# Clustered attention and a two-layer channel mix: the order of all steps written out as one list, on one core

## The chip, the cores and the metric

The kernel runs on one core of one Trainium2 chip. The metric is device time in microseconds (us) of one execution. The kernel before was timed three times. One more execution was recorded by the hardware profiler; every row of the profile below is of that execution. The engines are TensorE (PE, with its weight loads PEld), VectorE (DVE), ScalarE (ACT), GpSimd (POOL) and SyncE (SP), which here only issues DMAs.

## What is computed

Four batches, eight heads, 768 positions, head width 64, 16 centroids per head; then a mix over positions of rank 32 and a channel mix 512 to 2048 to 512. Cut to what matters:

```python
q_assign = argmax(normed(q) @ normed(centroids).T)       # 16 clusters, k the same
mask     = q_assign[..., :, None] == k_assign[..., None, :]
attn     = softmax(where(mask, 0.125 * q @ k.T, -1e9))
x        = (attn @ v), heads side by side                 # (4, 768, 512)
u        = x + (x.T @ U @ V).T
out      = u + relu(u @ w_ch1) @ w_ch2
```

U, V and the two weight matrices arrive as float64 bits and are joined into float32 on the chip.

## The kernel before

**Attention.** Sixteen steps i, one for each batch and pair of heads (four to a batch). For each: `load` brings q and k (tile R), `split_hi` (ACT) and `split_lo` (POOL or DVE) cut them into a high and a low half, `sims`, `largest` and `clusters` find each position's cluster, `clusters_T` (ACT, tile ohT) turns that into one-hot rows, and `place_clusters` writes these by eight DMAs from SP into the large tile `arena`, where they stand beside q and k as further rows of one matrix product. `rowmax` (L570 PE, L572 DVE) is a first pass over the scores for the row maxima, `rowmax_place` (ACT) puts these into `arena` by a DMA of its own queue (tile mT). Then come `scores` (L594 and L596 on PE, the exponential L599 on ACT), `weights` (L609, sums on POOL and DVE), `values` (L617, the weights times v, matmuls of the form 128*64), and `sums`, `sums_T`, `normalise`. After each fourth step come `mix_u`, `mix_sum`, `mix_v`.

**Channel mix.** `fetch_blocks` (L787) reads u back in blocks, `turn_blocks` (L793) transposes on DVE, `add_u` and `split_u` (L805) make operands; `convert` and `merge` (L219, L220, L222: three DVE instructions for each half tile, called "a conversion" below) join the weights' bits, `split_w` (L828) and `split_w2` (L837) cut them into halves, `stage_w` and `load_w2` bring stored ones back from DRAM. The first product is done with seven products instead of eight for each 2 by 2 block: `product(g, p)`, p = 0 to 6, six matmuls each (L854 to L856, tile ps_h), whose result DVE adds up (L862) or ACT copies (L866). `relu` (L892 DVE, L894 ACT) gives hh and hl, and `gemm2` (L1048 to L1050, tile y) multiplies by the second matrix, with `finish` after it. From group 16 on (the "phase") the second product is done with seven products too: `relu_home`, `add_h`, `split_h` (L922 DVE, L924 ACT), `product2` (L997 to L999, tile z), `combine2` (L1007), `output` (L1030, L1033 and a DMA).

**Order.** Tables of numbers (`times`, `mixes`, `stages`, `joins`, `mlp`, `phase`, `order0`, `paces`, `spots`) give every step a time in units of its own. `at` puts (time, step) into `plan`, the plan is sorted, and each step, when called, emits all its instructions, on all the engines that it uses, at this one place. `keep_order` then pins the order of emission on each engine. So each engine works through its instructions strictly in that order, and one that waits holds everything behind it on that engine.

**Buffers.** A rotating tile is taken from a pool with `bufs=2` or more; which buffer it is follows from the order of the calls.

**Semaphores of the DMAs.** The DMAs of SP and ACT draw from one set of eight completion semaphores in turn. They appear in the lists below as DMAHW0 to DMAHW7. A DMA whose semaphore is still held by an earlier DMA waits for that one to complete.

The places that the change and the prediction touch: `plan`, `at` and the last four lines of `clustered_attention_moe`; `merge`, `convert`; `product`; `place_clusters`, `rowmax_place`; `values`; `split_h`, `output`; `turn_blocks`, `fetch_blocks`; every `tile(...)` of a rotating pool.

## Time and profile before

| what | value |
|---|---|
| three timed runs, median (lowest to highest) | 1012.67 us (1010.91 to 1015.03) |
| the profiled execution, its own time | 1011.91 us |
| its span in the trace | 1009.5 us |
| its mean granted TensorE clock | 0.98 |
| busy: PE, PEld, DVE | 943.9 us (93%), 757.4 us (75%), 781.2 us (77%) |
| busy: ACT, POOL | 463.8 us (46%), 656.8 us (65%) |
| chain that ended last, by engine | PE 64%, DVE 13%, POOL 7%, DMA 6%, issue 4%, ACT 3% |

PE is busy for all but 65.6 us of the span. Matmuls are pipelined, so a busy PE is not a PE at its peak. The clock column gives the share of full speed that was granted; 0.50 is 1.2 GHz and 1.00 is 2.4 GHz. The list of waits says which engine stood still for whom, and the timeline of one engine shows in which order its instructions ran and what stood ahead of the one that was late.

### The profile page before, as it was taken

What the parts mean: (1) busy time and instruction counts of PE and PEld (TensorE: products, weight loads), DVE (VectorE), ACT (ScalarE), POOL (GpSimd) and SP (SyncE); (2) the same over time, 40 slices, a digit from 0 to 9 for tenths busy, and PEclk for the clock granted to TensorE, in tenths of its full rate; (3) what the DMA queues carried; (4) which work ended last, traced back from release to release, by engine and by line L of the source; (5) the groups of instructions that cost most, each with busy time, mean ns of one, the idle gap of its engine ahead of it and who ended that gap; (6) DMA issues with size and microseconds to landing.
All of it is one profiled execution on the core that took longest, in us unless ns stands there. A gap on an engine that the chain in (4) does not pass through costs nothing.

```text
span 1009.5 us, 14837 instructions
## 1 busy us (share of the span) xinstructions
PE 943.9 (93%) x5098; PEld 757.4 (75%) x5098; DVE 781.2 (77%) x1251; ACT 463.8 (46%) x680; POOL 656.8 (65%) x433
## 2 busy tenths in 40 slices
PE   7799999999999999999999899998798997999997
PEld 5566666666667666658888778887698887999996
DVE  5798888778887877567886767665777998588974
ACT  7355555565556545553433334432334453345530
POOL 6467776788678879975688887964723673035620
PEclk9899999999999999999999899999989999999999
DMA  7656656575656665037377765689476966777785
GB/s 199 149 134 173 167 145 189 154 195 148 191 145 178 167 158 126 1 65 205 128 254 256 250 211 196 243 272 257 165 215 152 214 196 185 229 157 164 236 252 136
DMA packets 169645, 183.13 MB, mean 181 GB/s; under 512 B 110426, under 2 KB 119252, under 8 KB 168548
## 3 DMA queue, kind: packets, MB, share of 16 engines
q1 hardware_dynamic: 136672, 156.21, 56.4%
q10 hardware_dynamic: 32900, 25.99, 8.1%
q8 instruction: 40, 0.66, 0.3%
q14 instruction: 33, 0.27, 0.1%
HBM read 112.72 MB, written 41.42 MB: 153 GB/s over the span
## 4 chain that ended last, share of the span: by engine, by line
PE 64%; DVE 13%; POOL 7%; DMA 6%; issue 4%; ACT 3%; SPq 2%; ACTq 1%; POOLq 0%; DVEq 0%
PE o_ps L617 12%; PE ps_max L570 7%; PE st L594 6%; PE st L596 6%; PE ps_h L854 4%; PE ps_h L856 4%; PE ps_h L855 4%; PE z L998 3%; PE z L999 3%; PE z L997 3%; PE y L1050 2%; PE y L1049 2%; PE y L1048 2%; POOL sums_w L820 2%; DVE m L572 2%
## 5 line engine op out<-in xcount | busy, mean ns | idle before, releaser
L609 POOL TENSOR_TENSOR T<-T,pr 128x768 f32<-128x768 f32 x120 | 222.7, 1856 | 52.4 <-DVE T L609 30.7
L572 DVE TENSOR_REDUCE m<-ps_max 128x1 f32<-128x384 f32 x372 | 186.5, 545 | 44.8 <-PE ps_max L570 43.2
L599 ACT ACTIVATE pr<-st 128x768 f32<-128x768 f32 x186 | 148.9, 812 | 74.9 <-PE st L596 63.1
L854 PE MATMUL ps_h<-arena,combos 128*128 128x384 f32 x352 | 122.3, 348 | 14.1 <-DVE rw_g L862 8.4
L617 PE MATMUL o_ps<-pr,vt 128*64 128x384 f32 x768 | 131.1, 490 | 0.7 <-DMA vt<-in_v 0.3
L856 PE MATMUL ps_h<-arena,combos 128*128 128x384 f32 x352 | 120.9, 344 | 5.3 <-POOL combos L944 4.0
L570 PE MATMUL ps_max<-arena 128*128 128x384 f32 x372 | 114.8, 374 | 7.4 <-DMA arena<-ohT 5.5
L855 PE MATMUL ps_h<-arena,combos 128*128 128x384 f32 x352 | 120.6, 343 | 0.5 <-DVE arena L805 0.5
L617 PEld LDWEIGHTS o_ps<-pr,vt 128*64 128x64 f32 x768 | 52.5, 137 | 66.2 <-issue 58.9
L594 PE MATMUL st<-arena 128*128 128x384 f32 x372 | 100.2, 350 | 1.3 <-ACT pr L599 1.3
L570 PEld LDWEIGHTS ps_max<-arena 128*128 128x128 f32 x372 | 67.9, 191 | 41.5 <-issue 14.4
L596 PE MATMUL st<-arena 97*128 97x384 f32 x372 | 95.9, 339 | 0.0
L609 POOL TENSOR_TENSOR T<-pr 128x768 f32<-128x768 f32 x30 | 56.5, 1885 | 46.5 <-ACT pr L599 46.5
L854 PEld LDWEIGHTS ps_h<-arena,combos 128*128 128x128 f32 x352 | 67.9, 193 | 23.5 <-DVE rw_g L862 9.2
L944 POOL TENSOR_TENSOR combos<-rw,combos 128x1024 fp32r<-128x1024 f32 x10 | 24.9, 2490 | 92.7 <-ACT combos L946 92.7
L1050 PE MATMUL y<-w,hl 128*128 128x512 f32 x192 | 78.0, 406 | 3.7 <-DVE hl L892 3.6
L1049 PE MATMUL y<-w,hh 128*128 128x512 f32 x192 | 77.4, 403 | 2.4 <-POOL w L837 2.4
L594 PEld LDWEIGHTS st<-arena 128*128 128x128 f32 x372 | 65.1, 189 | 16.4 <-issue 7.3
L1048 PE MATMUL y<-w,hh 128*128 128x512 f32 x192 | 76.1, 396 | 0.0
L894 ACT ACTIVATE hh<-c 128x768 fp32r<-128x768 f32 x32 | 27.1, 846 | 102.1 <-DVE c L862 100.9
L856 PEld LDWEIGHTS ps_h<-arena,combos 128*128 128x128 f32 x352 | 67.8, 192 | 7.6 <-POOL combos L944 5.7
L855 PEld LDWEIGHTS ps_h<-arena,combos 128*128 128x128 f32 x352 | 68.1, 193 | 4.6 <-DVE arena L805 1.0
(213 smaller groups left out, 2153.3 us busy)
## 6 DMA issues: line engine op xcount, KB each, us to landing
combos<-w_scr SPq DMA_DIRECT2D x112, 256.0 KB
R<-in_qk SPq DMA_DIRECT2D x32, 384.0 KB
arena<-arena SPq DMA_DIRECT2D x64, 192.0 KB
arena<-arena SPq DMA_DIRECT2D x31, 384.0 KB
late_rw<-in_w SPq DMA_DIRECT2D x20, 512.0 KB
u<-u_scr SPq DMA_DIRECT2D x96, 96.0 KB
rw<-w_scr SPq DMA_DIRECT2D x15, 512.0 KB
vt<-in_v SPq DMA_DIRECT2D x16, 384.0 KB
```

The lines of the kernel that those rows point to most:

```text
L570: nc.tensor.matmul(ps[:, 0:HS], x1[:, 0, g // 2, g % 2, t * P:(t + 1) * P], x1[:, 1, h, g % 2, :], start=True, stop=True)
L572: nc.vector.reduce_max(live["m2", i][:, h, u:u + 1], ps[:, 0:HS], axis=AX.X)
L594: nc.tensor.matmul(st[:, j, 0:HS], x1[:, 1, hk, j, ks], x1[:, 0, h, j, :], start=True, stop=False)
L596: nc.tensor.matmul(st[:, j, 0:HS], x2[0:97, 1, hk, j, ks], x2[0:97, 0, h, j, :], start=False, stop=True)
L599: nc.scalar.activation(pr, st[:, :, 0:HS], AF.Exp, scale=SCALE)
L609: eng.tensor_add(T, live["p", i, h, 0] if c == 1 else T, live["p", i, h, c])
L617: nc.tensor.matmul(o_ps[64 * j:64 * j + 64, 0:HS], vv[:, c, j, :], pr[:, j, :], start=(c == 0), stop=(c == NT - 1))
L854: nc.tensor.matmul(ps, ah[:, d], oh[:, d], start=(d == 0), stop=False)
L855: nc.tensor.matmul(ps, ah[:, d], ol[:, d], start=False, stop=False)
L856: nc.tensor.matmul(ps, al[:, d], oh[:, d], start=False, stop=(d == 1))
L1049: nc.tensor.matmul(y, hh[:, f, ts], w2[:, 1, f, :], start=False, stop=False)
L1050: nc.tensor.matmul(y, hl[:, f, ts], w2[:, 0, f, :], start=False, stop=(g in lasts and f == 1))
```

## The change

The time tables go. In their place stand `sequence`, a list of 4,334 step numbers, and `kept`, which holds for each rotating tile a string of buffer numbers. Steps that used more than one engine are written as generators that stop between engines (`@pieces(n)`, `yield`), and `list_work` writes all steps down in a plain order. The list then calls them, a piece at a time, in its own order. The operations and their counts are the same on every engine (4,552 matmuls on PE in both).

```diff
-times = {
-    "load0":           (-38.729, -44.925, -46.182,   None,   None, -82.544),
...
+kept = {
+    "R":
+        "0101010101010101010110101110100110",
...
+def pieces(n):
+
+    def mark(fn):
+        fn.pieces = n
+        return fn
+    return mark
...
+    def place(home, key, shape, dtype, name):
+
+        return home.tile(shape, dtype, name=name, tag=f"{key}{next(turns[key])}", bufs=1)
...
     def merge(rw, g, b, t):
 
         nc.vector.tensor_scalar(b, g, 3, None, op0=ALU.logical_shift_left)
+        yield
         nc.vector.scalar_tensor_tensor(out=b, in0=g, scalar=-0x80000000, in1=b,
                                        op0=ALU.bitwise_and, op1=ALU.bitwise_or)
+        yield
...
+    @pieces(3)
     def product(g, p):
...
-        ps = (work("ps_h") if g <= NG else pool["y"].tile([P, 512], F32, name="ps_h", tag="y"))[:, 0:HS]
+        ps = (work("ps_h") if g <= NG else place(pool["y"], "y", [P, 512], F32, "ps_h"))[:, 0:HS]
...
+        yield
+
         def combine(out, i0, i1, op=ALU.add):
...
+    def put(fn, *args):
+
+        count = getattr(fn, "pieces", 1)
+        plan.extend([fn(*args) if count > 1 else iter(lambda: fn(*args), 0)] * count)
...
-    plan.sort(key=lambda event: event[:2])
-    for _, _, fn, args in plan:
-        fn(*args)
+    list_work()
+    for k in sequence:
+        next(plan[k], None)
     keep_order(tc)
```

What the list does is seen in the engines' own orders. Three places follow. Line numbers differ between the two files: L862 is L1078 after, L922 is L1140, L219, L220 and L222 are L382, L384 and L387, L262 is L429.

**SP in the opening, around `place_clusters` of step 1** (ohT to `arena`); the second list begins at the same `load` of step 2, and R is q and k. Before:

```order
L380 DMA R_487<-in_qk 128x768 [waits DMAHW7_49,PE_49]
L262 DMA arena_124<-arena_124 32x1536 [waits DMAHW1_49,DMAHW0_49]
L262 DMA arena_124<-arena_124 32x1536 [waits DMAHW4_49]
L262 DMA arena_124<-ohT_502 16x384 [waits DMAHW2_49,Activation_49]
L262 DMA arena_124<-ohT_502 16x384 [waits DMAHW3_49]
L262 DMA arena_124<-ohT_502 16x384
L262 DMA arena_124<-ohT_502 16x384 [waits DMAHW5_49]
L262 DMA arena_124<-ohT_502 16x384 [waits DMAHW6_49]
L262 DMA arena_124<-ohT_502 16x384 [waits DMAHW7_49]
L262 DMA arena_124<-ohT_502 16x384 [waits DMAHW0_49]
L262 DMA arena_124<-ohT_502 16x384 [waits DMAHW1_49]
L380 DMA R_487<-in_qk 128x768 [waits DMAHW2_49]
```

After:

```order
L555 DMA R_468<-in_qk 128x768 [waits DMAHW4_49,PE_49]
L555 DMA R_468<-in_qk 128x768 [waits DMAHW5_49]
L429 DMA arena_124<-ohT_472 16x384 [waits DMAHW7_49,DMAHW6_49,Activation_49]
L429 DMA arena_124<-ohT_472 16x384
L429 DMA arena_124<-ohT_472 16x384 [waits DMAHW0_49]
L429 DMA arena_124<-ohT_472 16x384 [waits DMAHW1_49]
L429 DMA arena_124<-arena_124 32x1536 [waits DMAHW2_49]
L429 DMA arena_124<-arena_124 32x1536 [waits DMAHW4_49]
L429 DMA arena_124<-ohT_472 16x384 [waits DMAHW5_49]
L429 DMA arena_124<-ohT_472 16x384 [waits DMAHW6_49]
L429 DMA arena_124<-ohT_472 16x384 [waits DMAHW7_49]
L429 DMA arena_124<-ohT_472 16x384 [waits DMAHW0_49]
```

The first four writes of ohT, for the first half of step 1, now stand ahead of the two row copies of `place_queries`, which are between them and the second four. All eight together stand ahead of the next loads.

**DVE in the channel mix, around the conversion numbered 20** (L219, L220, L222 before; L382, L384, L387 after), which in the kernel before stands between the sums of `product(6, 2)` (tile rw_g) and `product(6, 3)` (tile rw_t); hl is the low half of `relu`. Before:

```order
L862 TENSOR_TENSOR c0_5034<-ps_h_5937,rw_g_5926 128x384
L862 TENSOR_TENSOR rw_g_5965<-ps_h_5958,rw_g_5926 128x384
L219 TENSOR_SCALAR joined_5197<-late_g_5196 128x512
L220 SCALAR_TENSOR_TENSOR joined_5197<-late_g_5196,joined_5197 128x512
L222 SCALAR_TENSOR_TENSOR joined_5197<-late_rw_5195,joined_5197 128x512
L862 TENSOR_TENSOR rw_t_5987<-ps_h_5980,rw_g_5965 128x384
L862 TENSOR_TENSOR c0_5034<-rw_t_5987,ps_h_6002 128x384
L892 SCALAR_TENSOR_TENSOR hl_6019<-c0_5034,hh_6018 128x768
L862 TENSOR_TENSOR rw_t_6029<-ps_h_6022,rw_g_5965 128x384
L862 TENSOR_TENSOR c1_5035<-ps_h_6022,rw_t_5987 128x384
```

After, from the same sum of `product(6, 2)` on:

```order
L1078 TENSOR_TENSOR rw_g_6005<-ps_h_5963,rw_g_5960 128x384
L1078 TENSOR_TENSOR rw_t_6035<-ps_h_6018,rw_g_6005 128x384
L1078 TENSOR_TENSOR c0_5066<-rw_t_6035,ps_h_6027 128x384
L1110 SCALAR_TENSOR_TENSOR hl_6059<-c0_5066,hh_6047 128x768
L1078 TENSOR_TENSOR rw_t_6068<-ps_h_6038,rw_g_6005 128x384
L1078 TENSOR_TENSOR c1_5067<-ps_h_6038,rw_t_6035 128x384
L382 TENSOR_SCALAR joined_5214<-late_g_5213 128x512
L1078 TENSOR_TENSOR c1_5067<-ps_h_6049,rw_t_6068 128x384
L384 SCALAR_TENSOR_TENSOR joined_5214<-late_g_5213,joined_5214 128x512
L387 SCALAR_TENSOR_TENSOR joined_5214<-late_rw_5212,joined_5214 128x512
```

The three instructions of the conversion moved behind four sums of group 6 and its first `relu`, and a sum of `product(6, 6)` stands between the first of the three and the second.

**DVE in the phase, around `split_h` of the operand t3** (tile h_t3, which the first `product2` of that operand needs); the transposes of c1 and the sums into u are `output`. Before:

```order
L1007 TENSOR_TENSOR c0_5034<-z_8089,z0_7418 128x384
L1007 TENSOR_TENSOR c0_5034<-z_8093,z0_7418 128x384
L922 TENSOR_TENSOR combos1_5033<-h_left_7417,combos1_5033 128x768
L1030 STREAM_TRANSPOSE c1_5035<-c0_5034 128x384
L805 TENSOR_TENSOR arena_124<-turned_127,arena_124 128x768
L1033 TENSOR_TENSOR u_7756<-c1_5035,u_7756 128x384
L1030 STREAM_TRANSPOSE c1_5035<-c0_5034 128x384
L1033 TENSOR_TENSOR u_7756<-c1_5035,u_7756 128x384
L922 TENSOR_TENSOR arena_124<-h_t3_7421,arena_124 128x768 x3
```

After:

```order
L1226 TENSOR_TENSOR c0_5066<-z_8065,z0_7406 128x384
L1140 TENSOR_TENSOR arena_124<-h_left_7405,arena_124 128x768
L1140 TENSOR_TENSOR arena_124<-h_t3_7409,arena_124 128x768
L1018 TENSOR_TENSOR arena_124<-turned_127,arena_124 128x768
L1140 TENSOR_TENSOR combos1_5065<-h_left_7405,combos1_5065 128x768
L1140 TENSOR_TENSOR arena_124<-h_t3_7409,arena_124 128x768 x2
L1251 STREAM_TRANSPOSE c1_5067<-c0_5066 128x384
L1018 TENSOR_TENSOR arena_124<-turned_127,arena_124 128x768
L1140 TENSOR_TENSOR arena_124<-h_left_7405,arena_124 128x768
```

The first of the three splits of h_t3 moved ahead of a split of u (L805 before, L1018 after), of the last split of h_left, and of all four instructions of `output`. 

The other moves of a size, in words. On DVE, `turn_blocks(2, 0, 2)` and `turn_blocks(2, 0, 3)` stood ahead of the sum of `product(14, 2)` and now stand behind `relu` of group 14's first half. The split of t1 (L805) and one `split_w` (L828) stood ahead of the sum of `product(15, 4)` and now stand behind it. The `fetch_blocks`, `turn_blocks` and `split_u` of batch 1 moved forward, from the beginning of the channel mix into the last attention steps. On PE, the runs of consecutive `values` matmuls are 59 instead of 33, the runs of `product` 69 instead of 98, and those of `gemm2` 62 instead of 92. On SP, nine of the loads of R and v stand nearer to the step that reads them: between the load of R for step 9's second half, for one, and its `sims` the order of emission has 113 matmuls before and 27 after. For the nine these numbers are 45 to 132 before and 20 to 49 after.

## Rows read from the trace of the kernel before

**Rows 1.** Windows of the span: us, busy us (instructions) by engine, clock, DMA share, GB/s.

```profile
0.00:50.00 50.00, 38.31 (x204) 25.44 (x205) 31.99 (x71) 27.36 (x58) 26.39 (x65) 0.93 0.70 174
50.00:425.00 375.00, 370.88 (x2164) 251.12 (x2164) 307.08 (x611) 207.12 (x310) 293.98 (x162) 1.00 0.58 153
425.00:475.00 50.00, 46.66 (x240) 32.34 (x239) 32.62 (x44) 23.63 (x34) 35.85 (x24) 0.97 0.48 111
475.00:760.00 285.00, 261.75 (x1245) 229.62 (x1244) 210.19 (x266) 106.90 (x139) 200.82 (x135) 0.96 0.69 223
760.00:1010.00 250.00, 226.26 (x1252) 218.87 (x1250) 199.37 (x263) 98.79 (x141) 99.74 (x48) 0.98 0.73 192
```

**Rows 2.** Waits of PE, 475 to 760: tile, line, releaser, us in total, times, longest.

```profile
PE ps_h L854 <- DVE rw_g L862: 8.4, 4, 4.0
PE ps_h L854 <- DVE c L862: 4.6, 2, 4.1
PE ps_h L854 <- DVE rw_t L862: 4.1, 1, 4.1
PE y L1050 <- DVE hl L892: 3.6, 4, 1.7
PE y L1049 <- POOL w L837: 2.4, 1, 2.4
```

**Rows 3.** Waits of PE, 760 to 1010: the first two and the last of seven.

```profile
PE z L998 <- DVE arena L922: 8.1, 4, 4.2
PE ps_h L856 <- POOL combos L944: 4.0, 4, 1.8
...
PE z L997 <- DMA combos<-w_scr: 0.5, 2, 0.3
```

**Rows 4.** Waits of PE, 0 to 50: the first.

```profile
PE ps_max L570 <- DMA arena<-ohT: 5.5, 1, 5.5
```

**Rows 5.** Waits of PE, 425 to 475: the first of seven.

```profile
PE ps_rep L670 <- ACT xu L666: 0.7, 1, 0.7
```

**Rows 6.** Waits of PE, 50 to 425: the first of six.

```profile
PE st L594 <- ACT pr L599: 1.3, 3, 0.7
```

**Rows 7.** Windows of the eight half-clock stretches: two of them, and their sum.

```profile
37.90:44.70 6.80, 5.07 (x13) 3.78 (x13) 4.39 (x9) 0.38 (x1) 0.00 (x0) 0.50 0.66 186
...
563.60:570.40 6.80, 5.56 (x16) 5.29 (x17) 5.72 (x9) 1.41 (x2) 6.41 (x8) 0.50 0.55 210
...
sum 37.50, PE 33.17 PEld 30.30 DVE 25.01 ACT 6.73 POOL 14.91; mean PE 4.15 PEld 3.79 DVE 3.13 ACT 0.84 POOL 1.86
```

**Rows 8.** Timeline of DVE, 553 to 568: start us, us, line, operation, [idle before].

```profile
557.13 1.64 DVE L219 TENSOR_SCALAR joined<-late_g 128x512 int32<-128x512 int32 x1 [2.04 <-ACT late_g L716]
...
564.24 0.55 DVE L862 TENSOR_TENSOR rw_t<-ps_h,rw_g 128x384 f32<-128x384 f32 x1
```

**Rows 9.** Line L222, the last third of a conversion: ns, shortest/median/longest.

```profile
L222 DVE SCALAR_TENSOR_TENSOR joined<-late_rw,joined x8: 692/1114/2758, 514.1 to 593.4; 128x512 int32<-128x512 int32 x8
```

**Rows 10.** Timeline of DVE, 694 to 705.

```profile
701.79 0.58 DVE L793 STREAM_TRANSPOSE turned<-u 128x384 f32<-128x384 f32 x1 [5.61 <-DMA u<-u_scr]
```

**Rows 11.** Waits of SP's DMA queue, 683 to 703.

```profile
SPq L787 <- DMA w_scr<-late_rw: 6.0, 1, 6.0
```

**Rows 12.** Timeline of SP, 27 to 42: eight issues, merged.

```profile
29.73 9.73 SPq L262 DMA_DIRECT2D arena<-ohT  x8
```

**Rows 13.** Waits of SP's DMA queue, 27 to 40.

```profile
SPq L262 <- DMA arena<-mT: 4.9, 1, 4.9
```

**Rows 14.** Timeline of PE, 201.5 to 204.

```profile
202.17 0.52 PE L570 MATMUL ps_max<-arena 128*128 128x384 f32 x2
202.62 1.83 PE L617 MATMUL o_ps<-pr,vt 128*64 128x384 f32 x10
```

**Rows 15.** Timeline of SP, 4.5 to 12.

```profile
4.74 0.58 SPq L380 DMA_DIRECT2D R<-in_qk  x1
```

**Rows 16.** Timeline of ACT, 10.5 to 13.

```profile
11.09 0.83 ACT L461 CAST arena<-R 128x768 fp32r<-128x768 f32 x1 [0.78 <-DMA R<-in_qk]
```

697 lines of the change are left out of this document (335 added, 362 removed), and 207 rows, old and new, of the table sequence.

## The prediction, as it was made before the run

> **What bounds the kernel now.** I read the windows of the span first [rows 1]. The reader is to see that PE is busy nearly throughout: 370.88 of 375 us in attention from 50 on, 261.75 of 285 in the channel mix, 226.26 of 250 in the phase. DVE, the next, has 307.08, 210.19 and 199.37 us there. So PE sets the time, and a reordering that adds and removes no operation can gain only where PE stands still, or where it runs at the lower clock. Second, the list of PE's waits, stage by stage, shows who ends them. In the channel mix five groups make 23.1 us, of which 17.1 are `product` waiting for DVE's sums [rows 2]. In the phase seven make 16.8, led by `product2` waiting for DVE's `split_h` with 8.1 and `product` waiting for POOL's combos with 4.0 [rows 3]. In the opening one wait of 5.5 stands out, for the one-hot rows' DMA [rows 4]. From 425 to 475 seven groups make 3.2 us [rows 5], and in the 375 us of attention six make no more than that, the first with 1.3 [rows 6]: there PE is simply full. Third, the granted clock. It is 0.50 (1.2 GHz, the lower of the two levels) in eight stretches of 37.5 us in all, each right behind a stall of PE; PE is busy for 33.17 us of them [rows 7]. Matmuls that took 33.17 us at half clock would take about half at full, so the low clock itself costs up to 16.6 us. A stall of 4 us therefore costs more than 4.
>
> **The change part by part.** The operations are the same, so no term is for work added or removed. The sum is made against the profiled execution's 1011.91 us, which lies 0.76 below the median of the three runs and 2.4 above its span; I let those 2.4 stand.
>
> *Channel mix, 475 to 760.* The pattern is one engine's queue: DVE works strictly in order, and a conversion of three instructions stands ahead of the sum that frees `product`'s buffer. From 557.13 to 564.24 the conversion holds DVE for 7.1 us [rows 8], and PE stands still for 4.1 of them, up to that sum [rows 2]. So PE could swallow 3.0 us of delay there and not 7.1. In the new order the three instructions come later and, at this one, with a sum between the first and the second. The longest instruction of that kind took 2.758 us [rows 9]: one alone lies within the 3.0. Two together, as the second and third here, can still cost up to 2.5 (twice 2.758 less 3.0), but at the shortest 0.692 nothing. At 701.79 DVE had waited 5.61 us for the DMA of u before `turn_blocks` [rows 10], and `product(14, 2)` was behind it; it now stands ahead. That DMA itself stays late, since SP's issue waited 6.0 for an earlier DMA's completion semaphore [rows 11]; what is late next is then the `split_u` behind the transpose, whose readers come later. The split of t1 and the `split_w` that stood ahead of `product(15, 4)` moved behind it too. Price of all that: 23.1 us of waits, and the low clock. Four of the eight stretches lie here, two of 6.8 and two of 3.4 us; in the first PE is busy for 5.56 of 6.80 [rows 7], at which share the four hold 16.7 busy us and cost half of that, 8.3. Together 31.4. What moved away is nearly everything that I traced a stall to, but each moved piece stands ahead of something else, and DVE is still busy for 74% of the stage. I take 22, about two thirds. Bounds: 31 (the whole), and 8 (only the two clean cases, 4.1 and 4.0, with no clock).
>
> One row speaks against taking all. The same instruction of a conversion took 0.692 us at the shortest and 2.758 at the longest [rows 9], and in the stretch where it was longest POOL was busy for 6.41 of 6.80 us [rows 7]. The Trainium skill, "SBUF — State Buffer", section "Who interferes with whom", says that a DVE instruction with two SBUF inputs contends with a GpSimd instruction that reads SBUF, and that the second to start blocks until the first is done. The trace agrees in its 0.692 against 2.758. By that rule moving the instruction does not make it short, and where the new place has POOL at work it may only move the stall. By the row of the 3.0 us that PE can swallow this term is 22, by the rule at its worst the lower bound, 8: that is the first rival below.
>
> *Phase, 760 to 1010.* Waits of 16.8 us [rows 3], and two half-clock stretches of 3.4 and 3.5 us, worth 2.8 at the same share: 19.6. The longest wait, 4.2 [rows 3], ends with the first `split_h` of t3, which had `output` and two splits ahead of it; it now goes ahead of them. What is late next is `output`, which nothing on PE reads. The POOL waits come from stored weights brought late; two of those loads now go ahead of block loads on SP. But DVE is busy for 80% of this stage [rows 1], so what is put back comes due soon. I take 12, or 60%. Bounds: 19 (nearly the whole) and 4 (the longest wait alone).
>
> *Opening, to 50.* SP's eight writes of one-hot rows take from 29.73 on 9.73 us to issue [rows 12], because one waits 4.9 us for the semaphore of a DMA of ACT's queue [rows 13], and PE loses 5.5 [rows 4]. In the new order the first half stands earlier and no DMA of ACT stands between. To this belongs a half-clock stretch of 6.8 us with 5.07 busy [rows 7], worth 2.5. Together 8.0; ACT's reordered copies may give 1 more or less. I take 6.5; bounds 10 (with 2 from the earlier ACT work) and 2 (the next load holds it).
>
> *425 to 475.* The chain from `sums` to `mix_v` keeps its order. Of 3.2 us of waits [rows 5] and a half-clock stretch of 3.4 us, worth 1.4, I take 1; bounds 5 and 0.
>
> *Attention.* A run of `values` matmuls has another tile form. Entering one, two `rowmax` matmuls take 0.45 us from start to start of the next (202.17 to 202.62) [rows 14] where 2164 matmuls in 375 us make 0.17 each [rows 1], or 0.35 for two: 0.1 more, and about as much at the exit. 26 more runs by 0.2 are 5 us lost, and nothing hides it, since PE is full there. At most 1 us of the waits [rows 6] is won back: +4; bounds 0 and 9 (twice the price, less 1).
>
> The rest (batch 1's blocks fetched in attention, where DMA and DVE have room; buffers named by hand) costs nothing as long as they land in time; DVE's 82% of the stage [rows 1] is the cover, and without it the third rival comes in.
>
> Sum: 1011.91 − 22 − 12 − 6.5 − 1 + 4 = 974.4; with the 0.76 to the median, 975.
>
> **The rivals.** *Gains given back*, about 1000. DVE's pieces remain long beside POOL, and each stall reappears at a neighbour. For it: 0.692 to 2.758 us for one instruction [rows 9], and POOL busy for 200.82 of 285 us [rows 1]. Against it: a single piece lies within the 3.0 us that PE can swallow. With the lower bounds of the two large terms, 8 and 4, 5 from the opening and 4 lost in attention: 1012.7 − 13 = 1000.
>
> *Nearly all waits go*, about 953. The list is one for each single instruction, so it can set every one; then 31 + 19 + 8 + 2 are won, and `values` costs nothing: 1012.7 − 60 = 953. Against it: each batch's chain of DMA, transpose and split has a length of its own.
>
> *Slower: loads too late*, about 1023. The mechanism is SP's queue in attention. Nine loads of R and v stand much nearer to their readers: 20 to 49 matmuls ahead, at 0.17 us [rows 1] 3.4 to 8.3 us, against 45 to 132 matmuls before. A load of R took 6.35 us from issue to its reader's start (4.74 to 11.09, the reader waiting) [rows 15, 16], and a semaphore held SP for 6.0 once [rows 11]. With both, 12.35 less the 3.4 to 8.3 leaves 4 to 9 us. If each of the nine is late by 5 and PE's clock falls behind each (6.8 us at half, busy 5.56 [rows 7], so 2.8 lost), 9 by 7.8 are 70 us. The 37.5 forecast gain would turn into a loss of 33, and with half of the nine hit no gain is left; it decides from about five of the nine on. At two thirds of the price, 47, the time is 1012.7 − 37 + 47 = 1023. Against it: in attention PE waited for a DMA hardly at all [rows 6], DMA share is 0.58, and PE has `rowmax`, `scores` and `values` of other steps in its order.
>
> **How the numbers follow.** Forecast, 960 to 990: 0.50. Gains given back, 990 to 1007: 0.21. Nearly all, 946 to 960: 0.16. No difference, since part of both happens: 0.05. Slower: 0.08. A measurement of this kernel tells 0.5% (5 us) from no change. Faster by more than that is 0.50 + 0.21 + 0.16 = 0.87, within 0.05, slower 0.08. The range leaves out the slower case and the edges: 948 (all upper bounds, 31 + 19 + 10 + 5, give 1012.7 − 65) to 1004 (the lower bounds, 8 + 4 + 2 + 0 less 5, give 1012.7 − 9).
>
> **What would show it.** In the new trace PE's waits from the beginning of the channel mix to the end should be about 14 us instead of 39.9, and the half-clock stretches some three or four instead of eight. The wait for one-hot rows in the opening should be gone or under 1 us. The attention stretch should be 3 to 5 us longer than before, without a new wait. DVE's busy time should stay near 781 us; if its conversions are as long as before and PE still waits under 15 us, the first rival is out. The prediction is wrong if PE's list of waits in attention shows `arena` or `vt` waiting for DMAs with more than 10 us, or if the waits of the channel mix keep over 15 us under other names.

## The result: 971.53 us, and where the 42 us came from

The changed kernel takes **971.53 us** (median of four, 971.04 to 975.41) where the kernel before takes 1013.85 on the same chip: ratio 0.9593, 95% interval 0.9557 to 0.9629. The forecast was 975, within 948 to 1004. The profiled execution took 971.04, with a span of 969.2 (before 1009.5) and a mean clock of 0.987 (before 0.98).

First the profile page of the changed kernel: busy time and share of the span by engine, and the chain that ended last.

```profile
PE 934.8 (96%) x5098; PEld 747.3 (77%) x5098; DVE 767.0 (79%) x1251; ACT 461.9 (48%) x680; POOL 642.1 (66%) x433
...
PE 82%; DVE 7%; DMA 5%; issue 2%; ACT 2%; POOL 2%; SPq 0%; ACTq 0%; DVEq 0%; POOLq 0%
```

PE's busy time fell by only 9 us (from 943.9), the span by 40. So it is PE's standing still that went: the chain that ended last now runs through PE for 82% of the span instead of 64, through DVE for 7 instead of 13.

Line numbers have moved: `product` L854 to L856 is now L1068 to L1070, its sums on DVE L862 are L1078, its copies on ACT L866 are L1082, `split_h` L922 is L1140, `values` L617 is L805, `rowmax` L570 and L572 are L750 and L755, a conversion L219, L220, L222 is L382, L384, L387.

**The length of each stage.** Windows at fixed times don't compare, since everything came earlier. The same four pieces of work do: the first matmul of `values`, the last of `mix_v`, the last of `gemm2` and the last of `product2`. These are rows of lines, first of before, then of after; behind the count stand shortest, median and longest ns, then the first and the last start in us.

```profile
L617 PE MATMUL o_ps<-pr,vt x768: 486/486/538, 45.2 to 442.2; 128*64 128x384 f32 x192
L679 PE MATMUL ps_h<-x,v x24: 391/400/508, 155.0 to 460.0; 96*128 96x512 f32 x24
L1050 PE MATMUL y<-w,hl x192: 387/397/632, 470.1 to 748.8; 128*128 128x512 f32 x192
L999 PE MATMUL z<-arena,combos x176: 333/334/522, 810.2 to 1003.2; 128*128 128x384 f32 x176
```

```profile
L805 PE MATMUL o_ps<-pr,vt x768: 486/486/903, 39.3 to 447.7; 128*64 128x384 f32 x192
L881 PE MATMUL ps_h<-x,v x24: 391/401/792, 150.2 to 466.2; 96*128 96x512 f32 x24
L1271 PE MATMUL y<-w,hl x192: 387/397/558, 472.6 to 728.8; 128*128 128x512 f32 x192
L1217 PE MATMUL z<-arena,combos x176: 333/334/346, 783.7 to 962.9; 128*128 128x384 f32 x176
```

| stage | before | after | measured | predicted |
|---|---|---|---|---|
| opening, to the first `values` | 45.2 | 39.3 | −5.9 | −6.5 |
| attention, from there to the last `mix_v` | 414.8 | 426.9 | +12.1 | +3 (+4, and −1 for 425 to 475) |
| channel mix, to the last `gemm2` | 288.8 | 262.6 | −26.2 | −22 |
| phase, to the last `product2` | 254.4 | 234.1 | −20.3 | −12 |
| sum | | | −40.3 | −37.5 |

The sum is close partly by luck, since the errors of the terms cancel: channel mix and phase together won 12 us more than forecast, attention lost 9 more, and the opening won 0.6 less.

No work moved across these borders: attention has 2360 PE instructions in both kernels, the channel mix 1249 and 1243, the phase 1315 and 1322. But the same order does not always give the same length. The experiments on single mechanisms that leave a stage as it is in the changed kernel have, together with it, 38.2 to 40.2 us in the opening, 425.1 to 427.5 in attention, 262.6 to 265.0 in the channel mix and 232.0 to 235.8 in the phase. A difference of 2 to 4 us in one stage of one execution is therefore no evidence by itself.

**PE's waits after.** Waits of PE by tile, line and releaser (us in total, times, longest), from 470 to 740, the channel mix:

```profile
PE ps_h L1068 <- ACT rw_g L1082: 3.5, 2, 2.6
PE y L1271 <- DVE hl L1110: 1.3, 1, 1.3
PE ps_h L1068 <- DVE c L1078: 0.8, 3, 0.3
```

This is all of it: 5.6 us where it was 23.1 [rows 2]. `product` waiting for DVE's sums fell from 17.1 to 0.8. From 740 to the end, the phase, the first two of four rows:

```profile
PE ps_h L1068 <- DVE c L1078: 2.5, 1, 2.5
PE z L1216 <- DVE combos L1140: 0.6, 1, 0.6
...
```

All four are 3.6 us in place of 16.8 [rows 3]; both leaders of that list, 8.1 for `split_h` and 4.0 for POOL's combos, are gone. In the opening the wait of 5.5 for the one-hot rows [rows 4] is gone too. But attention and its end have new ones. The first row below is the longest from 47 to 425, the others lead the list from 425 to 470:

```profile
PE st L783 <- DMA arena<-ones: 2.4, 1, 2.4
...
PE ps_h L881 <- DVE xt L883: 2.0, 2, 1.2
PE ps_sumT L830 <- ACT sums L823: 0.9, 1, 0.9
...
```

**The clock.** Behind the opening three stretches at half clock are left, with 17.0 us, where seven with 30.7 were (eight with 37.5, less the opening's 6.8) [rows 7]. One of 6.9 us lies in the opening itself. Windows of all four, in the columns of [rows 1]:

```profile
11.80:18.70 6.90, 6.18 (x35) 5.66 (x34) 3.67 (x8) 5.03 (x8) 2.54 (x7) 0.51 0.72 166
418.00:424.80 6.80, 6.28 (x19) 3.07 (x19) 3.67 (x3) 1.51 (x2) 6.80 (x4) 0.50 0.39 139
465.80:472.60 6.80, 6.02 (x16) 4.96 (x16) 4.23 (x7) 1.72 (x2) 3.97 (x4) 0.50 0.76 262
701.30:704.70 3.40, 3.40 (x11) 3.21 (x11) 2.78 (x3) 1.19 (x2) 3.32 (x3) 0.50 0.84 328
```

The second and the third stand right behind new waits. Only the second lies in attention, whose last `mix_v` starts at 466.2; of the third 0.4 us do. So the waits and the clock explain a good half of attention's 12.1 us, and the section on the prediction adds it up.

### The profile page after: what moved, and what is told of

Its sections match the earlier page's. It is cut to its first block, busy times and chain, and to the rows that moved or that the text cites. A ratio compares the mean times of both kernels' runs of the same rounds, so it can differ in the third digit from the quotient of the medians.

```text
span 969.2 us, 14666 instructions
## 1 busy us (share of the span) xinstructions
PE 934.8 (96%) x5098; PEld 747.3 (77%) x5098; DVE 767.0 (79%) x1251; ACT 461.9 (48%) x680; POOL 642.1 (66%) x433
## 4 chain that ended last, share of the span: by engine, by line
PE 82%; DVE 7%; DMA 5%; issue 2%; ACT 2%; POOL 2%; SPq 0%; ACTq 0%; DVEq 0%; POOLq 0%
PE o_ps L805 13%; PE ps_max L750 7%; PE ps_h L1068 7%; PE ps_h L1070 7%; PE ps_h L1069 7%; PE st L781 7%; PE st L783 6%; PE z L1216 4%; PE z L1215 4%; PE z L1217 4%; PE y L1271 4%; PE y L1270 3%; PE y L1269 3%; DVE m L755 2%; PE ps_sum L820 1%
## 5 line engine op out<-in xcount | busy, mean ns | idle before, releaser
L755 DVE TENSOR_REDUCE m<-ps_max 128x1 f32<-128x384 f32 x372 | 189.2, 549 | 45.2 <-PE ps_max L750 43.0
L805 PE MATMUL o_ps<-pr,vt 128*64 128x384 f32 x768 | 138.8, 499 | 0.0
L1068 PE MATMUL ps_h<-arena,combos 128*128 128x384 f32 x352 | 120.8, 343 | 8.2 <-ACT rw_g L1082 3.5
L1070 PE MATMUL ps_h<-arena,combos 128*128 128x384 f32 x352 | 119.3, 339 | 0.0
L1069 PE MATMUL ps_h<-arena,combos 128*128 128x384 f32 x352 | 119.2, 339 | 0.0
L750 PE MATMUL ps_max<-arena 128*128 128x384 f32 x372 | 113.0, 368 | 2.4 <-DVE m L755 1.6
L805 PEld LDWEIGHTS o_ps<-pr,vt 128*64 128x64 f32 x768 | 50.3, 138 | 65.2 <-issue 60.0
L750 PEld LDWEIGHTS ps_max<-arena 128*128 128x128 f32 x372 | 65.8, 188 | 42.0 <-DVE m L755 18.1
L1068 PEld LDWEIGHTS ps_h<-arena,combos 128*128 128x128 f32 x352 | 66.9, 190 | 15.3 <-DVE c L1078 5.3
L1270 PE MATMUL y<-w,hh 128*128 128x512 f32 x192 | 76.0, 396 | 0.0
L1269 PE MATMUL y<-w,hh 128*128 128x512 f32 x192 | 75.2, 392 | 0.0
L783 PEld LDWEIGHTS st<-arena 97*128 97x128 f32 x372 | 68.4, 190 | 3.5 <-issue 2.7
L1069 PEld LDWEIGHTS ps_h<-arena,combos 128*128 128x128 f32 x352 | 67.0, 190 | 2.3 <-issue 0.2
L1070 PEld LDWEIGHTS ps_h<-arena,combos 128*128 128x128 f32 x352 | 66.9, 190 | 0.0
```

The source lines that it names most:

```text
L750: nc.tensor.matmul(ps[:, 0:HS], x1[:, 0, g // 2, g % 2, t * P:(t + 1) * P], x1[:, 1, h, g % 2, :], start=True, stop=True)
L755: nc.vector.reduce_max(live["m2", i][:, h, u:u + 1], ps[:, 0:HS], axis=AX.X)
L783: nc.tensor.matmul(st[:, j, 0:HS], x2[0:97, 1, hk, j, ks], x2[0:97, 0, h, j, :], start=False, stop=True)
L805: nc.tensor.matmul(o_ps[64 * j:64 * j + 64, 0:HS], vv[:, c, j, :], pr[:, j, :], start=(c == 0), stop=(c == NT - 1))
L1068: nc.tensor.matmul(ps, ah[:, d], oh[:, d], start=(d == 0), stop=False)
L1069: nc.tensor.matmul(ps, ah[:, d], ol[:, d], start=False, stop=False)
```

## New waits in attention: a semaphore on SP, and a piece in DVE's queue

The wait for `ones` at 418 comes from SP. Its timeline from 394 to 420 (start, us, line, operation), and then what its DMA queue waited for there:

```profile
394.77 21.24 SPq L998 DMA_DIRECT2D u<-u_scr  x16
416.06 0.81 SPq L429 DMA_DIRECT2D arena<-ones  x1
```

```profile
SPq L998 <- DMA arena<-mT: 11.9, 1, 11.9
```

Sixteen block loads of batch 1, which the new order fetches early, stand ahead of `place_ones` of step 15. One of them shares a completion semaphore with the row-max DMA (mT) of ACT's queue and waits 11.9 us for it; nobody needs that block yet, but `ones` stands behind it. PE's timeline shows the end:

```profile
415.48 0.61 PE L781 MATMUL st<-arena 128*128 128x384 f32 x2 [0.24 <-ACT pr L787]
418.52 0.98 PE L783 MATMUL st<-arena 97*128 97x384 f32 x2 [2.44 <-DMA arena<-ones]
```

2.44 us of waiting, then the 6.8 us at half clock shown above, in which PE was busy for 6.28; half of that, 3.1, is lost. One misplaced 1x12x128 load costs 5.5 us where it happens, in this execution. The stretch behind it is not always there: other kernels below wait 2.2 to 2.5 us at the same place and have 6.8 us at half clock behind it (x_phase_pe), 3.4 (e_open, e_conv) or none (e_split, e_output). It is the mechanism of the prediction's slower rival, at one place instead of five.

A second new wait is in DVE's row of `mix_v` additions (L883, two instructions merged in each row):

```profile
462.29 1.29 DVE L883 TENSOR_TENSOR xt<-ps_h,xt 128x512 f32<-128x512 f32 x2
463.50 1.46 DVE L1110 SCALAR_TENSOR_TENSOR hl<-c,hh 128x768 fp32r<-128x768 f32 x1
464.88 1.27 DVE L883 TENSOR_TENSOR xt<-ps_h,xt 128x512 f32<-128x512 f32 x2
```

A `relu` of the channel mix (hl, 1.46 us) stands between additions that PE's next `mix_v` matmul waits for (2.0 us for `xt`, 0.5 before), and the half-clock stretch from 465.8 on follows. That the `relu` is its cause is not shown: e_best below moves it behind the additions and still waits 1.6 us for `xt`, with 6.8 us at half clock there, and the old order itself has 6.8 us there in x_all_old (463.9 to 470.7) where the kernel before has 3.4.

## Experiments that put whole stages back

Two theories were to be told apart. The **order** theory says that the time changed only through the order, and each stage's gain belongs to the order in that stage. Its rival is that the rewritten code (generators, buffers named by hand) or one coupled effect across stages carries the gain. All kernels here are written through the new list; pieces of the list are put back into the order in which the kernel before issues its steps, and buffers follow. Diffs show a few rows of one engine's order, against the changed kernel. Ratios are against the kernel before, measured beside each; the changed kernel has 0.9593.

**All back** (x_all_old), on every engine; DVE at a conversion:

```diff
+SCALAR_TENSOR_TENSOR hl<-c,hh 128x768
+TENSOR_TENSOR rw_t<-ps_h,rw_g 128x384
+TENSOR_TENSOR c<-ps_h,rw_t 128x384 x2
+TENSOR_SCALAR joined<-late_g 128x512
+SCALAR_TENSOR_TENSOR joined<-late_g,joined 128x512
 SCALAR_TENSOR_TENSOR joined<-late_rw,joined 128x512
-TENSOR_TENSOR c<-ps_h,rw_t 128x384
```

> The changed kernel's code with a list that puts every engine back into the order of the kernel before, on all engines and stages; the numbers of the buffers are chosen anew for that order. If the order alone carries the gain (first theory), the time is that of the kernel before within 0.5%, about 1013. If the single-engine pieces, the fixed buffers or the way waits are put down carry a part (rival), it comes out below 1008.

Measured 1013.49 us, ratio 1.0004 (0.9987 to 1.0021). The old waits are back as well, in the opening (first row) and the phase (second):

```profile
PE ps_max L763 <- DMA arena<-ohT: 5.4, 1, 5.4
...
PE z L1229 <- DVE arena L1153: 8.4, 6, 4.2
```

So the code is free, and the order carries all of the gain.

**New, then old** (x_new_old): the new order until the first product of group 1, the old one from there, that is, in channel mix and phase. DVE behind the cut:

```diff
-TENSOR_SCALAR w2f<-late_g 128x512 x2
+SCALAR_TENSOR_TENSOR hl<-c,hh 128x768
 TENSOR_TENSOR c<-rw_t,ps_h 128x384
...
 TENSOR_TENSOR c<-ps_h,rw_t 128x384
+TENSOR_SCALAR w2f<-late_g 128x512
 SCALAR_TENSOR_TENSOR w2f<-late_g,w2f 128x512
```

> The new order up to the first product of group 1 of the channel mix, the order of before from there, on all engines. By the terms of the prediction (opening 6.5 and transition 1 won, values 4 lost) it comes out 3.5 under the kernel before, about 1010. By the two traces (time that PE loses beyond its matmuls: opening 5.5 less, 50 to 400 2.3 more, 400 to 475 10.5 more) it comes out 5 to 9 slower than the kernel before, about 1020.

Measured 1016.8, ratio 1.0031 (1.0008 to 1.0054): opening and attention by themselves lose a little, where the terms of the prediction made them win 3.5.

**Old, then new** (x_old_new): the reverse. ACT just behind the cut:

```diff
 CAST x<-ps_rep 96x512
+CAST w<-w2f 128x1024
 ACTIVATE hh<-c 128x768
-CAST combos<-rw 128x3x256
-CAST arena<-turned 128x768 x2
 CAST combos<-sums_w 128x4x256
+CAST combos<-rw 128x3x256
+CAST arena<-turned 128x768 x5
 ACTIVATE hh<-c 128x768
```

> The reverse: the order of before up to the first product of group 1, the new order from there, on all engines. By the terms of the prediction (22 and 12) it is 34 under the kernel before, about 980. By the two traces (63.5 us lost by PE after 475 before, 15.2 after) it is 45 or more under, about 966, and faster than the changed kernel itself by about 6.

Measured 999.6, ratio 0.9866 (0.9833 to 0.9899). At the cut stands one wait that neither kernel has:

```profile
PE ps_h L1081 <- ACT rw_g L1095: 28.3, 2, 26.2
```

ACT has five `split_u` copies of batch 1 in a row there, which wait for transposes of blocks that the new order would have fetched during attention. So the second half leans on the first by the early fetch: batch 1's blocks must be there when the new channel mix begins. Past it this run is like the changed kernel (phase 232.1 us).

**New, old phase** (x_new_phase_old): the new order until the first product of group 16, the old one after it. PE, with counts in brackets:

```diff
-MATMUL z<-arena,combos 128x384 (x48)
+MATMUL z<-arena,combos 128x384 (x36)
 MATMUL z<-combos,combos 128x384 (x6)
 MATMUL z<-combos 128x384 (x6)
-MATMUL z<-arena,combos 128x384 (x24)
-MATMUL z<-combos,combos 128x384 (x6)
-MATMUL z<-arena,combos 128x384 (x12)
-MATMUL z<-combos,combos 128x384 (x6)
```

> The new order up to the first product of group 16, where the phase begins, the order of before from there, on all engines. By the prediction's term the phase is worth 12: 971.5 + 12 = 983. By the two traces (PE's loss in this stage 26.5 us before, 5 after) it is worth 21: 992. With the 1016.8 of the run that has the old order from group 1 on, the difference to it is the channel mix: 33 by the first, 24 by the second.

Measured 1001.4, ratio 0.9894 (0.9858 to 0.9929), 29.9 us above the changed kernel and 9 more than the slower of the two expectations. By the same four pieces of work, in the profiled execution of each:

| kernel | opening | attention | channel mix | phase |
|---|---|---|---|---|
| before | 45.2 | 414.8 | 288.8 | 254.4 |
| after | 39.3 | 426.9 | 262.6 | 234.1 |
| x_all_old | 47.3 | 417.0 | 289.0 | 255.3 |
| x_new_old | 37.8 | 425.1 | 289.9 | 255.2 |
| x_old_new | 45.2 | 417.1 | 298.8 | 232.1 |
| x_new_phase_old | 37.9 | 431.9 | 272.9 | 255.3 |

The columns go by the order of their own stage: the opening is 45 to 47 us with the old order and 38 to 39 with the new, attention 415 to 417 and 425 to 432 (the 431.9 has a wait of 3.2 us for a row maximum that the changed kernel lacks), the phase 254 to 255 and 232 to 234. In the channel mix the old order takes 289 to 290; the two values between are the stall at the cut (298.8) and one of 6.5 us that ends at 622 in x_new_phase_old, where DVE waits 8.1 us for a DMA into `w_scr`. With these exceptions the order theory holds stage by stage, and the early fetch is a link across stages.

## Experiments on single mechanisms

**Conversions put together** (e_conv). Is it the position of DVE's three instructions that won the channel mix? Thirteen of the 20 conversions stand together again, ahead of the sums that they stood ahead of before. Only DVE's order changes:

```diff
-TENSOR_TENSOR rw_g<-ps_h,rw_g 128x384
 TENSOR_SCALAR joined<-late_g 128x512
-TENSOR_TENSOR u<-y,u 128x512
 SCALAR_TENSOR_TENSOR joined<-late_g,joined 128x512
+SCALAR_TENSOR_TENSOR joined<-late_rw,joined 128x512
+TENSOR_TENSOR rw_g<-ps_h,rw_g 128x384
+TENSOR_TENSOR u<-y,u 128x512
```

> The changed kernel with the three instructions of a conversion put back together, directly ahead of the sum of product that followed them in the kernel before, for the 13 of 20 conversions where their inputs allow it (17, 18, 20 and 23 go ahead of 8 to 10 instructions by this). If a conversion ahead of a sum is what stalled PE (first theory), waits of PE for L862's successor come back, 4 us for a place with its low clock behind it, at two or three places: 8 to 15 us, 980 to 986. If PE's own new order gives enough slack (rival), under 3 us.

Measured 1001.06, ratio 0.9888 (0.9864 to 0.9912), 29.5 us above the changed kernel: more than the whole gain of the stage, 26. Waits of PE from 470 to 740:

```profile
PE ps_h L1080 <- DVE c L1090: 14.8, 7, 6.0
PE ps_h L1080 <- DVE rw_t L1090: 5.3, 1, 5.3
PE ps_h L1080 <- DVE rw_g L1090: 4.1, 2, 3.3
PE ps_h L1080 <- ACT rw_g L1094: 2.5, 1, 2.5
```

The three DVE rows are the 17.1 us of [rows 2], back and grown to 24.2, and the granted clock of this window is 0.94, against 0.99 after. So the mechanism is shown: conversions ahead of the sums stall PE. That it costs more than the stage had won is a sign that old DVE pieces also fit badly into PE's new order.

The rival "gains given back" rests on the instruction's own duration. Its shortest and longest didn't change. Line L387 of the changed kernel, the last third of a conversion, in the columns of [rows 9]:

```profile
L387 DVE SCALAR_TENSOR_TENSOR joined<-late_rw,joined x8: 679/812/2779, 517.9 to 596.7; 128x512 int32<-128x512 int32 x8
```

679 to 2779 ns, as before (692 to 2758); the median fell from 1114 to 812. It is a DVE instruction with two SBUF inputs beside a busy POOL. The Trainium skill ("SBUF — State Buffer", section "Who interferes with whom") says that such an instruction contends with a GpSimd instruction that reads SBUF; the trace is in line with that by its 679 against 2779. The reordering did not make the long ones go away. What changed is what stands behind them. At conversion 20 a sum (L1078, 572.14) stands between the first third (L382, 570.53) and the other two. At others none does. DVE's timeline at the conversion with the longest third, and PE's first matmul that then waits:

```profile
584.38 0.82 DVE L382 TENSOR_SCALAR joined<-late_g 128x512 int32<-128x512 int32 x1
585.12 1.49 DVE L1110 SCALAR_TENSOR_TENSOR hl<-c,hh 128x768 fp32r<-128x768 f32 x1
586.53 0.68 DVE L384 SCALAR_TENSOR_TENSOR joined<-late_g,joined 128x512 int32<-128x512 int32 x1
587.25 2.78 DVE L387 SCALAR_TENSOR_TENSOR joined<-late_rw,joined 128x512 int32<-128x512 int32 x1
589.95 0.55 DVE L1078 TENSOR_TENSOR c<-ps_h,rw_t 128x384 f32<-128x384 f32 x1
...
590.55 0.45 PE L1068 MATMUL ps_h<-arena,combos 128*128 128x384 f32 x1 [0.25 <-DVE c L1078]
```

A whole conversion and a `relu`, 5.6 us, stand between two sums here, and PE waits 0.25 us for the second: until then it had `gemm2` and another product in its order. Four of the 20 conversions stand whole between two sums like this; in the kernel before all 20 did. So the 3.0 us that PE could swallow at one place of the kernel before [rows 2, 8] are no measure for other places, and short pieces are not what saves PE. What counts is which sum the conversion delays and what PE has to do meanwhile. How much of this PE's own new order gives was not tested in this stage.

**PE's order in the phase put back** (x_phase_pe). All other engines keep the new order; on PE 152 of the 237 steps from the first product of group 16 stand elsewhere, and 43 buffers follow:

```diff
-MATMUL z<-arena,combos 128x384 (x24)
-MATMUL z<-combos,combos 128x384 (x6)
-MATMUL z<-arena,combos 128x384 (x12)
-MATMUL z<-combos,combos 128x384 (x6)
-MATMUL z<-arena,combos 128x384 (x24)
+MATMUL z<-arena,combos 128x384 (x36)
 MATMUL z<-combos,combos 128x384 (x12)
 MATMUL z<-arena,combos 128x384 (x36)
```

> The changed kernel with PE's order alone put back from the first product of group 16 on (152 of 237 steps stand elsewhere); DVE, ACT, POOL and SP keep the new order, and 43 buffers are chosen anew for it. In the old order PE finishes one operand's product2 before the next, in the new it begins the next one's first matmuls ahead of the last ones' end. If this interleaving is what hides the splits of the next operand (theory after the run with the outputs put back, which lost nothing), most of the phase's 21 us comes back as PE's waits for split_h and combine: 10 to 20 us, 982 to 992. If the gain lies in the orders of DVE, SP and ACT (the prediction's theory), under 4 us come back.

Measured 992.3, ratio 0.9797 (0.9771 to 0.9823), 20.8 us above the changed kernel. By the four pieces of work the phase takes 251.1 us, so 17.0 of the 20.3 us that it had won are lost again; the channel mix, whose end the edit touches, takes 267.2 instead of 262.6. Waits of PE from 735 to 975, the first three of six:

```profile
PE z L1227 <- DMA combos<-w_scr: 5.0, 5, 1.9
PE ps_h L1080 <- DVE c L1090: 3.8, 3, 1.8
PE z L1228 <- DVE combos L1152: 2.3, 4, 0.7
```

The six make 14.2 us, nearly the 16.8 of [rows 3], but they are other waits. The 8.1 for `split_h` into `arena` and the 4.0 for POOL's combos, which led the old list and which the expectation wanted back, stay away (0.7 and none). The new orders of DVE and SP take those two away even under PE's old order, as the prediction said; stored weights (0.5 before) and sums of `product` come late instead, and little is gained. So the gain of the phase needs PE's own new order. Why is argued, not shown: it lets PE begin the next product of `product2` before the last is through, so that a stored weight or a split that comes a little late may find PE at work on something else. The rival is that the other engines' new orders simply don't fit PE's old one. PE's new order alone was not run, since it contradicts the old order of the other engines.

**The reason that the prediction gave for the phase** (e_output). The transpose and the sum of one `output` go back ahead of the first `split_h` of t3, and a split of u ahead of a later one; DVE only:

```diff
 TENSOR_TENSOR arena<-h_left,arena 128x768
+STREAM_TRANSPOSE c<-c 128x384
+TENSOR_TENSOR u<-c,u 128x384
 TENSOR_TENSOR arena<-h_t,arena 128x768
...
 TENSOR_TENSOR arena<-h_left,arena 128x768
+TENSOR_TENSOR arena<-turned,arena 128x768
 TENSOR_TENSOR combos<-h_t,combos 128x768
```

> The changed kernel with four DVE instructions of the phase put back: the transpose and the sum of one output and the split of t3 ahead of the splits of h_t3 (as in the kernel before), and one split of t1. If they were what made PE wait 4.2 us for the first split of h_t3 (first theory), PE's wait for L1140 comes back with 2 to 4 us and a half-clock stretch: 974 to 978. If PE's order in the phase now gives slack for it (rival), under 1.5 us.

Measured 973.25, ratio 0.9603 (0.9574 to 0.9631): 1.7 us above the changed kernel, within the noise. PE's waits for L1140's successor are 1.7 us (0.6 after). As a test of the theory it is weak: the pair put back takes 1.1 us ahead of the first `split_h` of t3 (803.23 to 804.30), where in the kernel before `output` and two splits took 7.3 (835.51 to 842.77). It shows slack for 1.1 us, and leaves open whether the position of `output` won the 4.2.

**Longer runs of `values`** (e_joined) and **shorter ones** (e_split). The new order has 59 runs of the 128*64 form instead of 33, and the prediction priced a run at 0.2 us. Joined to 41 runs, split to 82; PE only, one place each:

```diff
 MATMUL ps_max<-arena 128x384 x2
-MATMUL o_ps<-pr,vt 64x384 x10
 MATMUL ps_sumT<-ident,sums 128x128 x3
-MATMUL o_ps<-pr,vt 64x384 x2
+MATMUL o_ps<-pr,vt 64x384 x12
 MATMUL ps_max<-arena 128x384 x3
```

```diff
-MATMUL ps_max<-arena 128x384 x2
-MATMUL o_ps<-pr,vt 64x384 x12
+MATMUL ps_max<-arena 128x384
+MATMUL o_ps<-pr,vt 64x384 x6
+MATMUL ps_max<-arena 128x384
+MATMUL o_ps<-pr,vt 64x384 x6
```

> The changed kernel with the values matmuls of a head joined into one run where the exponentials' buffers allow it: 41 runs instead of 59, nothing else moved. By the price of the prediction (0.2 us for each extra run, on a full PE) it gains 18 by 0.2 = 3.6 us: 968. If the switch costs nothing (rival), or if the late runs hold buffers that ACT then waits for, no gain or a loss.

> The changed kernel with 23 more cuts in the runs of values matmuls (82 runs instead of 59): each time one rowmax or scores step that stood beside a run moves into its middle, nothing else. By the price in the prediction (0.2 us for each extra run) it loses 23 by 0.2 = 4.6 us: 976. If an extra run costs nothing that lasts, because PE in this stage keeps DVE's pace anyway (rival, after the run with joined runs lost 16), under 1.5 us.

Joined: 987.65, ratio 0.9749 (0.9724 to 0.9774), 16 us slower where the price alone made it 3.6 faster. Attention takes 442.9 us instead of 426.9. Waits of PE from 47 to 450 in e_joined, the first two of nine:

```profile
PE ps_max L762 <- DVE m L767: 5.6, 7, 1.9
PE ps_oT L855 <- DVE m L767: 5.3, 2, 4.1
```

A matmul of attention takes PE 0.17 us on average [rows 1], the maximum of a `rowmax` takes DVE 0.55:

```profile
L755 DVE TENSOR_REDUCE m<-ps_max 128x1 f32<-128x384 f32 x372 | 189.2, 549 | 45.2 <-PE ps_max L750 43.0
```

Short runs of `values` between the `rowmax` matmuls keep PE at DVE's pace. When they are joined, `rowmax` matmuls come closer together and DVE falls behind: of the waits from 47 to 450, 14.6 us are for its maxima (tile m), against 1.5 in the changed kernel from 47 to 425. So the 26 extra runs were not only a cost.

Split: 978.15, ratio 0.9658 (0.9625 to 0.9690), 6.6 us slower for 23 more runs, all of it in attention (433.4), with PE's waits hardly changed. That is 0.29 us a run; with the two intervals it may be 0.1 to 0.5. It agrees with the 0.2 that the prediction worked out from [rows 14].

**The opening's writes** (e_open). On ACT the first mT DMA moves ahead of a `split_hi`, and the writes of one-hot rows are listed behind it:

```diff
 ACTIVATE mT<-ps_mT 6x128
+DMA arena<-mT 1x6x128
 CAST arena<-R 128x768
 ACTIVATE pr<-st 128x384
-DMA arena<-mT 1x6x128
```

> The changed kernel with only the opening's writes of one-hot rows put back: the DMA of the row maxima on ACT's queue is issued ahead of all eight writes of step 1, with place_queries between, as in the kernel before. If the wait for that DMA's semaphore was the cause of PE's 5.5 us (first theory), 5 to 8 us come back: 977 to 980. If the opening's gain came from ACT's earlier copies (rival), under 2 us come back.

Measured 970.05, ratio 0.9575 (0.9551 to 0.96): no difference, and no answer on the wait either. SP's own order came out unchanged, the one-hot writes did not wait, and the edit so did not rebuild what [rows 13] shows. It did show the link between the queues. SP's next copy into `arena` waited for that mT DMA, first in the changed kernel, then in e_open:

```profile
SPq L429 <- DMA arena<-mT: 3.8, 1, 3.8
```

```profile
SPq L441 <- DMA arena<-mT: 0.3, 1, 0.3
```

ACT's DMA went out 2.8 us earlier (34.15 to 31.36), and SP's wait shrank by 3.5. As SP came to this copy 1.6 us earlier too, not all of the 3.5 can be put down to the move.

For the opening itself there is the cut, not a single edit: 5.5 and 5.4 us of waiting for `arena<-ohT` in the old order (before, x_all_old), none before 50 us in any kernel with the new. SP's timeline of the changed kernel shows how:

```profile
27.16 2.48 SPq L429 DMA_DIRECT2D arena<-ohT  x4
29.68 1.22 SPq L429 DMA_DIRECT2D arena<-arena  x2
30.95 2.50 SPq L429 DMA_DIRECT2D arena<-ohT  x4
```

The eighth write is out at 33.45 instead of 39.46 [rows 12].

**`ones` ahead of the block loads** (e_ones). SP only:

```diff
 DMA u<-u_scr 32x24x32 x8
-DMA u<-u_scr 32x24x32 x16
 DMA arena<-ones 1x12x128
+DMA u<-u_scr 32x24x32 x16
 DMA rw<-w_scr 128x1024
```

> The changed kernel with one DMA moved: place_ones of step 15 is issued on SP ahead of the block loads of batch 1, behind which it stood and which waited 11.9 us for the semaphore of ACT's DMA of row maxima. If that queue is the cause of PE's stall of 2.4 us at 416 and of the half-clock stretch behind it (first theory), both go: 4 to 6 us, 966 to 968. If the stall is only handed to the next wait (rival), under 1.5 us.

Measured 969.5, ratio 0.9574 (0.9548 to 0.9599). The stall and its half clock are gone; the window from 400 to 425 reads

```profile
400.00:425.00 25.00, 24.73 (x136) 16.03 (x135) 19.82 (x25) 15.82 (x23) 23.56 (x12) 1.00 0.55 86
```

with 24.73 us busy at clock 1.00. Attention is 3.3 us shorter (423.6), the channel mix 2.4 longer (265.0, within the spread of that stage), and the total is 2 us lower, with overlapping intervals. The 3.3 are less than the 5.5 because a half-clock stretch from 36.4 to 43.2, which in the changed kernel lies at 11.8 in the opening, now reaches 4.4 us into attention and costs 2.2. The cause of the wait is shown, its worth in the whole only bounded.

**Six moves together** (e_best). `ones` as above; the `relu` behind the `mix_v` additions; ACT's copy of a product ahead of a `split_u` that waits for a transpose; twelve `out_y` DMAs on ACT cut in two around a `relu_home`; one sum ahead of another `relu_home`; the mT DMA of e_open. The rows on DVE and ACT:

```diff
-TENSOR_TENSOR xt<-ps_h,xt 128x512 x2
+TENSOR_TENSOR xt<-ps_h,xt 128x512 x6
 SCALAR_TENSOR_TENSOR hl<-c,hh 128x768
-TENSOR_TENSOR xt<-ps_h,xt 128x512 x4
...
+TENSOR_TENSOR c<-rw_t,ps_h 128x384
 SCALAR_TENSOR_TENSOR arena<-c,arena 128x384
 TENSOR_TENSOR combos<-rw,combos 128x3x256
-TENSOR_TENSOR c<-rw_t,ps_h 128x384
...
-CAST arena<-turned 128x768
 COPY rw_g<-ps_h 128x384
-CAST arena<-turned 128x768
+CAST arena<-turned 128x768 x2
...
-DMA out_y<-u 32x12x32 x12
+DMA out_y<-u 32x12x32 x8
 ACTIVATE arena<-c 128x384
+DMA out_y<-u 32x12x32 x4
```

> The changed kernel with six single moves: place_ones of step 15 ahead of batch 1's block loads (SP); the low half of relu(0,0) behind the last sum of mix_v (DVE); the copy of product(15,0) ahead of a split of batch 2's u (ACT), which PE waited 2.6 us for; an output DMA behind relu_home(0,1) (ACT) and the sum of product(24,4) ahead of relu_home(0,3) (DVE), behind which PE waited 2.5; and the DMA of the opening's row maxima ahead of a split (ACT). Each takes away a wait in the trace of the changed kernel: 5 + 1.5 + 2.6 + 2.5 us and the low clock behind them, together 10 to 16: 956 to 962. If the waits are handed on (rival), 966 to 970.

Measured **964.04** (963.06 to 965.37), ratio 0.9518 (0.9492 to 0.9543), faster than both kernels: 7.5 us below the changed one, 48 below the one before, and a little short of what was expected. Mean clock 0.994; the half clock behind the opening is down from three stretches (17.0 us) to two with 10.2, one of 3.4 from 713.8 and this one:

```profile
457.80:464.60 6.80, 5.46 (x15) 4.65 (x16) 6.51 (x8) 1.00 (x3) 4.46 (x4) 0.50 0.72 255
```

It is as long as the one that stood at 465.8, though the `relu` no longer stands between the `mix_v` additions.

By stages it has 37.2, 421.7, 264.6 and 231.9 us: 2.1 won in the opening, 5.2 in attention, 2.2 in the phase, and 2.0 given back in the channel mix. Only attention's share is clear of the spread of its stage. The moves were found from the waits of the changed kernel, as this document reads them.

## Why the prediction was right, step by step

**What bounds it: right.** PE sets the time; what was won is PE's standing still and the low clock behind it. All PE waits of the span sum to 57.5 us before and 27.3 after, and those from the channel mix to the end to 9.2, where 14 were forecast from 39.9. Three half-clock stretches behind the opening, and one in it, stand against the three or four forecast.

**Channel mix, −22: right mechanism, size 26.** The two-thirds rule was cautious; nearly all of the 31 bound, 26, was won. e_conv shows that DVE's positions carry it: with 13 conversions joined again the stage takes 293.6 us. It shows them necessary, not that they alone suffice. One step of the reasoning fails: that a single piece of up to 2.758 us is safe because it lies within the 3.0 that PE could swallow. In the changed kernel 5.6 us stand ahead of a sum and cost 0.25.

**Phase, −12: right direction, mechanism incomplete, size 20.** The step that fell short is "it now goes ahead of them": `output` on DVE and stored loads on SP as the causes. In x_phase_pe, with DVE and SP in their new order, the waits that the prediction named do go, but others come, and only 3.3 of the 20.3 us are won. The prediction looked at the engines that PE waited for and not at PE's own order, without which the rest wins little. Whether `output` won the 4.2 us stays open, since e_output put back 1.1 of 7.3 us. The upper bound for the stage, 19, was about what came.

**Opening, −6.5: right**, 5.9 and without the wait. The half-clock stretch that was to go with it has not gone for good: 6.9 us of it lie at 11.8 in the changed kernel, and 3.4 or 6.8 us between 35 and 44 in seven of the later ones that have the new opening. That it is the missing ACT DMA between the writes rests on SP's timeline and the cut, not on an edit of its own.

**425 to 475, −1: wrong sign.** "The chain keeps its order" is not true of DVE, where a `relu` came in among the `mix_v` additions. Waits from 425 to 470 are 6.6 us (3.2 before, 425 to 475), and the half-clock stretch grew from 3.4 to 6.8 us. How much of this is the `relu` stays open: e_best moved it, and the wait for `xt` fell by 0.4 us only, the stretch not at all.

**Attention, +4: the price was right, the list was not whole.** Of the stage's 12.1 us, PE stands still for 3.5 more and is busy for 8.6 more; these are the windows of before and after, in the columns of [rows 1]:

```profile
45.20:460.00 414.80, 407.52 (x2360) 272.29 (x2360) 333.18 (x646) 226.80 (x338) 321.90 (x179) 1.00 0.56 145
```

```profile
39.30:466.20 426.90, 416.08 (x2360) 269.39 (x2359) 346.55 (x657) 229.14 (x345) 327.58 (x183) 0.99 0.58 148
```

Of the 3.5, `ones` is 2.4. Of the 8.6, the half clock is 3.3 (3.1 behind `ones`, 0.2 at the end). That leaves 5.3 for 26 runs, 0.2 each, which is the price of the forecast; e_split has 0.29. In e_best, without the wait for `ones`, attention is still 6.9 us longer than before; less 1.1 of standing still and 0.5 of half clock this is again 5.3. The forecast's "without a new wait" was wrong. "Nothing hides it" missed that short runs also keep PE at DVE's pace, which e_joined shows at 16 us.

**DVE's busy time** was to stay near 781 us and fell to 767.0. Most of the fall is in the phase: 206.5 us before, 187.9 after, with the two-input splits of h_left down from a mean of 1640 ns to 1260. That alone did not win the phase, for x_phase_pe has 185.0 there and little of the gain.

**The rivals.** *Gains given back* falls: long DVE instructions stay, the last third with 2.78 us at worst, and PE's waits in the channel mix are 5.6 us all the same. *Nearly all waits go* was true of channel mix and phase, not of attention; e_best at 964 is half of the way from 975 to its 953. *Loads too late* has the right mechanism, SP held by an ACT DMA's semaphore, here for 11.9 us, but in a load of `ones` rather than in R or v, and once. It cost 5.5 at that place, where 7.8 was assumed for one. The slow edge of the range, 1004, takes 5 for attention where that term's own bound is 9; with 9 it would be 1008.
